# The last four heads' k carried in the padding of the other groups, gathered by GpSimd DMAs, with the loads of w_in on GpSimd and the work in a new order

## The chip, the core and the metric

The kernel runs on one core of one Trainium2 chip. The core has a matrix engine (TensorE, PE in the profile), a vector engine (VectorE, DVE), a scalar engine (ScalarE, ACT), GpSimd (POOL) and SyncE (SP), which here only issues DMAs; 16 DMA engines move the data. The engines run side by side and wait for each other by semaphores. The metric is the device time of one execution in microseconds (us), as the median of several runs.

## What is computed

One token sequence of 2048 tokens with 448 channels (bf16) goes through a block with local attention and then a gated MLP whose gate mixes over the tokens:

```python
qkv = layernorm(x) @ wqkv                    # 448 x 1344; q, k, v of 16 heads, 28 wide
# token s attends to s, s-2, ..., s-14 (8 places, dilation 2)
h = x + softmax(q k^T / sqrt(28)) v @ wo
z = gelu(layernorm(h) @ w_in)                # 448 x 1792
z1, z2 = z[:, :896], layernorm(z[:, 896:])
g = w_sp @ z2 + b_sp                         # w_sp is 2048 x 2048, over the tokens
out = h + (z1 * g) @ w_out                   # 896 x 448
```

## The kernel before

**Stages.** x comes in six loads, is normalised (VectorE: statistics `st`, aggregate `mv`, the product `xn`; GpSimd: the reciprocal root `rs`) and transposed to `xhT`, channels down the partitions: for the first four blocks of 128 tokens on TensorE (`xT0` to `xT3`, copied out of PSUM by `xe`), for the rest by transposing DMAs from SP. From `xhT` TensorE makes q and k (`qk`) and the values (`v`). The attention runs in 18 blocks of some 112 queries: logits (`lg`, two jobs j = 0, 1 of eight heads), exponentials on ScalarE (`ex`), a product with a mask on VectorE (`mk`, line 804), the weighted sum (`o`), its normalisation (`rc`, `om`) and a transposing DMA back (`oT`). Then come the projection (`y`), h, its layer norm, `z2` and `z1`, and from about 121 us on the product with w_sp (`g`, line 950) and the one with w_out (`wo`, line 974).

**q and k.** They are made transposed, in `qkT`: 128 partitions, 8 columns (`gg`) of 2048 tokens. Column 2g holds q and column 2g+1 holds k of the heads 4g to 4g+3; each head has 32 partitions, of which 28 are its channels and 4 are padding. The weights for it, `wqk`, are laid out the same way: copies `wp` (line 514, the helper `move`) put 28 of every 32 columns in place from the raw weights `wraw`, which come in three loads (`wq_0` to `wq_2`), and a GpSimd `memset` (line 678) clears the padding. The tokens are cut in six tiles `QT` of 128, 128, 256, 512, 512 and 512. For each tile and each group g the product `qk{tile}_{g}` makes the two columns 2g and 2g+1 together:

```python
WK = [(0, 1, 2), (0, 3, 2)]
FK = [(0, 2, 3), (0, 1, 3)]
HK = [(1, 0), (2, 64)]
```

The 448 channels are three full chunks of 128 (six matmuls for the two columns, jobs F) and half a chunk of 64 (two matmuls, job H). The two halves use different rows of TensorE and run at the same time. `qe{tile}_{g}` copies the two columns out of PSUM to `qkT`, on ScalarE or VectorE. The logits read them per head:

```python
ins = e.matmul(psum[:, c:c + nq], qkT[p:p + DH, 2 * g + 1, k0:k0 + NK],
               qkT[p:p + DH, 2 * g, t0:t0 + nq], start=True, stop=True,
               tile_position=(p, 0))
```

with p = 32(2j + i), i = 0, 1: job j reads the heads 2j and 2j+1 of every group.

**Order.** Each piece of work is a job with its engine. `ORDER` lists all jobs by number; each engine runs its own jobs in that order, and a wait holds everything behind it on the same engine. `BANK` gives the PSUM bank of each job that needs one, `ON` the engine of each copy. Job 930 (the last number) is a filler: a matmul on constant data (line 989) that keeps TensorE busy while the first data come in. In the order before, SP issues x0, x1, wq_2, wq_0, wq_1, x2, x4, ..., then transposes (about 1.3 us each) with the eight loads of `w_in` between them, then the loads of w_sp. GpSimd runs the setup, the `rs` pairs and small copies `od`.

Of the kernel before, what the change touches and what calls it, by code (L numbers as in the profile page):

```python
# [5 lines left out]
S_TOK = 2048  # L6
D = 448
NHEAD = 16
DH = 28
# [16 lines left out]
ORDER = [1, 114, 23, 28, 5, 930, 930, 29, 4, 930, 930, 24, 930, 2, 930, 930, 3, 37, 25, 930, 39, 930, 6, 930, 930, 40, 930, 9,  # L26
# [65 lines left out]
WLH = [4, 4, 8, 9, 18, 1, 4, 12, 24, 4, 14, 34, 6, 22, 21, 26]  # L92
GRES = 1
WARMT = 9.0
COLD = 6.4
FIRST = [(0, 1), "q", (1, 2), (2, 4), "v", (4, 8), (8, 12), (12, 16), "o"]
LN1G = [(0, 1), (1, 1), (2, 2), (4, 4), (8, 4), (12, 4)]
NF2 = 1
WK = [(0, 1, 2), (0, 3, 2)]
OFF = [0, 128, 192, 320]  # L100
FK = [(0, 2, 3), (0, 1, 3)]
HK = [(1, 0), (2, 64)]
QT = [(0, 128), (128, 256), (256, 512), (512, 1024), (1024, 1536), (1536, 2048)]

# [942 lines left out]
```

## Time and profile before

| | us |
|---|---|
| median of three runs | 242.99 (242.45 to 243.13) |
| the profiled execution | 243.36 |
| its span, first to last instruction | 241.6 |
| TensorE busy | 234.5 |
| VectorE busy | 148.9 |
| ScalarE busy | 92.5 |
| GpSimd busy | 33.3 |

The granted clock of TensorE was full (0.999) over the span. In the page, busy shares over the span come first, then 40 equal slices with one digit per slice (9 is 90% or more), then the DMA queues, then the chain that ended last: from the last instruction back, at each step to what released it. Groups of instructions follow, one line each: engine, operation, output and inputs, shape, count, total busy time, the mean of one in ns, and the idle time before them with what ended it. A row of the timeline has the start, the length, the engine and what ran, and in brackets how long the engine had been idle and what ended that. Rows for DMA issues give the engine that issues, the size and the time from issue to landing. Matmuls are pipelined: the duration of one (379 ns at 512 columns) is longer than the distance to the next.

### The profile page before, as it was taken

To read this page: it belongs to the slowest core of one execution; us is meant where nothing else is said; L and a number is where in the kernel's file an instruction comes from. 1 tells how busy PE (TensorE), PEld (TensorE's weight loads), DVE (VectorE), ACT (ScalarE), POOL (GpSimd) and SP (SyncE) were. 2 spreads that over 40 slices of the span, in tenths; PEclk is the share of its full clock that TensorE was granted. 3 is DMA by queue.
4 is the path that set the end of the run, shared out by engine and by line. 5 is a ranking of instruction groups with operands and counts; after the bars stand their busy time and mean duration, and the time that the engine had idled before them with its cause. 6 is when DMAs were issued, how large, how long until landed. Compare 5 with 4: busy or idle time off the path is not lost.

```text
span 241.6 us, 4270 instructions
## 1 busy us (share of the span) xinstructions
PE 234.5 (97%) x1742; PEld 115.9 (48%) x1759; DVE 148.9 (62%) x321; ACT 92.5 (38%) x116; POOL 33.3 (14%) x76
## 2 busy tenths in 40 slices
PE   7899999999999999999999999999999999999995
PEld 5665454554555554444444444444444444444443
DVE  4899987999886988798793143043109232245264
ACT  4687577884898887859440000000000000000000
POOL 6332202003250210131451000000000000000000
PEclk9999999999999999999999999999999999999999
DMA  6943354536749496889999990000000001100112
GB/s 171 341 120 69 65 109 97 133 87 158 164 87 132 90 136 126 174 137 180 188 199 209 187 171 0 3 0 0 0 3 19 19 1 49 49 0 0 38 60 76
DMA packets 66394, 23.23 MB, mean 96 GB/s; under 512 B 58694, under 2 KB 66246, under 8 KB 66374
## 3 DMA queue, kind: packets, MB, share of 16 engines
q1 hardware_dynamic: 66304, 22.95, 45.8%
q8 instruction: 14, 0.23, 0.4%
q14 instruction: 6, 0.05, 0.1%
q10 hardware_dynamic: 70, 0.00, 0.0%
HBM read 6.84 MB, written 1.84 MB: 36 GB/s over the span
## 4 chain that ended last, share of the span: by engine, by line
PE 92%; DVE 2%; DMA 2%; ACT 1%; SPq 1%; issue 1%; DVEq 0%
PE psum L950 40%; PE psum L498 38%; PE psum L974 9%; PE psum L789 3%; PE psum L813 3%; DMA wraw<-in_A_wqkv_dram 2%; DVE st L616 1%; SPq L529 1%; ACT V L514 0%; ACT E L798 0%; DVE wqk L514 0%; DVE xn L627 0%; DVE mv L618 0%; DVE srg L981 0%; DVE qkT L514 0%
## 5 line engine op out<-in xcount | busy, mean ns | idle before, releaser
L959 DVE TENSOR_TENSOR ub<-psum,bb 128x512 bf16<-128x512 f32 x28 | 19.2, 689 | 56.6 <-PE psum L950 56.1
L950 PE MATMUL psum<-wsp_hi,z2p 128*128 128x512 bf16 x219 | 49.9, 379 | 0.3
L798 ACT ACTIVATE E<-psum 128x896 bf16<-128x896 f32 (+2 forms) x36 | 31.7, 932 | 8.2 <-PE psum L789 8.2
L950 PEld LDWEIGHTS psum<-wsp_hi,z2p 128*128 128x128 bf16 x224 | 21.9, 98 | 26.0
L498 PE MATMUL psum<-xhT,wqk 128*128 128x512 bf16 (+5 forms) x186 | 27.3, 307 | 1.5 <-DVE wqk L514 0.5
L950 PE MATMUL psum<-wsp_lb,z2p 128*128 128x512 bf16 x109 | 25.5, 379 | 0.1
L950 PE MATMUL psum<-wsp_la,z2p 128*128 128x512 bf16 x109 | 25.0, 379 | 0.2
L498 PE MATMUL psum<-w_in,hnT 128*128 128x448 bf16 (+1 forms) x128 | 24.6, 353 | 0.0
L498 PE MATMUL psum<-hnT,w_in 128*128 128x512 bf16 (+1 forms) x112 | 23.8, 380 | 0.0
L974 PE MATMUL psum<-w_out,z1p 128*128 128x448 bf16 (+1 forms) x119 | 22.8, 341 | 0.0
L616 DVE BATCH_NORM_STATS2 st<-x_tm 128x6 f32<-128x448 bf16 x32 | 18.8, 612 | 1.8 <-DMA x_tm<-in_A_x_dram 1.7
L804 DVE TENSOR_TENSOR E<-E,maskb 128x1792 bf16<-128x1792 bf16 (+2 forms) x18 | 19.4, 1092 | 0.7 <-ACT E L798 0.7
L876 DVE BATCH_NORM_STATS2 st<-z2p 128x6 f32<-128x448 bf16 x32 | 18.5, 607 | 1.7 <-ACT z2p L872 1.1
L498 PEld LDWEIGHTS psum<-xhT,wqk 128*128 128x128 bf16 (+1 forms) x192 | 12.7, 97 | 12.9 <-issue 4.1
L981 DVE TENSOR_TENSOR srg<-psum,x_tm 128x448 bf16<-128x448 f32 (+1 forms) x17 | 9.9, 594 | 13.3 <-PE psum L974 7.8
L950 PEld LDWEIGHTS psum<-wsp_la,z2p 128*128 128x128 bf16 x112 | 10.9, 98 | 13.2
L950 PEld LDWEIGHTS psum<-wsp_lb,z2p 128*128 128x128 bf16 x112 | 11.0, 98 | 13.2
L611 POOL TENSOR_TENSOR rs<-rs,negh 128x2 f32<-128x2 f32 (+2 forms) x22 | 16.9, 770 | 1.8
L610 POOL TENSOR_SCALAR rs<-mv 128x2 f32<-128x2 f32 (+2 forms) x22 | 7.7, 352 | 66.3 <-DVE mv L618 47.1
L974 PEld LDWEIGHTS psum<-w_out,z1p 128*128 128x128 bf16 x119 | 11.6, 98 | 10.3
L498 PEld LDWEIGHTS psum<-w_in,hnT 128*128 128x128 bf16 (+1 forms) x128 | 10.4, 97 | 11.8 <-issue 3.0
L917 ACT ACTIVATE z1p<-psum 128x1024 bf16<-128x1024 f32 x14 | 14.1, 1021 | 4.5 <-PE psum L498 4.5
(53 smaller groups left out, 228.6 us busy)
## 6 DMA issues: line engine op xcount, KB each, us to landing
w_in<-in_B_w_in_dram SPq DMA_DIRECT2D x8, 224.0 KB, 3.2
out_dram<-srg SPq DMA_DIRECT2D x16, 112.0 KB, 1.8
x_tm<-in_A_x_dram SPq DMA_DIRECT2D x3, 448.0 KB, 7.1
w_out<-in_B_w_out_dram SPq DMA_DIRECT2D x1, 784.0 KB, 5.6
bb<-in_B_b_sp_dram SPq DMA_DIRECT2D x1, 512.0 KB, 5.2
wraw<-in_A_wqkv_dram SPq DMA_DIRECT2D x2, 224.0 KB, 2.9
wraw<-in_A_wqkv_dram SPq DMA_DIRECT2D x1, 448.0 KB, 5.7
wv<-in_A_wqkv_dram SPq DMA_DIRECT2D x2, 224.0 KB, 6.9
```

Source lines behind the costliest of these rows:

```text
L498: ins = e.matmul(o, w, x, start=g not in seen, stop=left[g] == 0, **kw)
L610: [(lambda e: e.tensor_single_scalar(A, mv[:, m:m + n, 1], EPS, ALU.add), r_mv[k][m:m + n], [rr]), (lambda e: e.tensor_tensor(R, A, negh[: ...
L611: (lambda e: e.tensor_tensor(R, A, negh[:, 0:1].to_broadcast([128, n]), ALU.pow), [rr, r_negh], r_rs[k][m:m + n])],
L616: [(lambda e: e.bn_stats(st[:, m, :], src), [rsrc], [r_st[k][m]])], dve_t(D))
L798: return e.activation(o, i, AF.Exp, scale=SCALE)
L804: return e.tensor_tensor(a, a, maskb[:, 0:1, pad:pad + nq].to_broadcast([NK, NHEAD, nq]), ALU.mult)
L876: [(lambda e, m=m, k=k: e.bn_stats(st3[:, m, k, :], z2p[:, m, D * k:D * (k + 1)]), [r_z2[m]], [r_st[2][m]])], dve_t(D))
L917: return e.activation(o, i, AF.Gelu_apprx_tanh)
L950: ins = e.matmul(psv(tk), z2p[:, s, 128 * fc:128 * fc + 128], w[:, 512 * (tc % 2):512 * (tc % 2) + 512], start=(s == 0), stop=(s == NB - 1))
L959: [(lambda e, tc=tc, s=s, tk=tk: e.tensor_tensor(ub[:, s, :], psv(tk), bb[:, 512 * tc:512 * tc + 512], ALU.add), [r_bb], [r_ub[s]])], dve_ ...
L974: ins = e.matmul(psv(tk, 0, c1 - c0), z1p[:, fc, 128 * m:128 * m + 128], w_out[:, fc, c0:c1], start=(fc == 0), stop=(fc == FC7 - 1))
L981: [(lambda e, m=m, s=s, tk=tk, c0=c0, c1=c1: e.tensor_tensor(srg[:, s, c0:c1], psv(tk, 0, c1 - c0), x_tm[:, m, c0:c1], ALU.add), [r_x[m]], ...
```

## The change

1. The k of the last four heads (group 3, 112 channels) is no longer made in a column of its own. The padding of the other seven columns has 7 x 4 x 4 = 112 places; the weights of those channels are put there by five new copies `wx0` to `wx4` (each for one chunk of input channels), so the products of q and k of the seven columns make them as well. The clearing of the padding on GpSimd goes; a clearing of one half chunk of column 6 on VectorE (`wpad`) comes.
2. Group 3 has then only its q column. Its product `qk{tile}_3F` is four full matmuls, the one over a half chunk having zeros in the other half of its weights; `qe{tile}_3` copies one column.
3. `qkT`'s column 7 is filled by 20 DMAs `kg{i}_{h}`, issued by GpSimd: for each of five groups of tiles `KG` (the first two tiles together) and each of the four rows of heads h, 4 partitions by 7 columns become 28 partitions of column 7. They wait for all copies `qe` of their tiles. Job j of the logits waits for the gathers of h = 2j and 2j+1.
4. The eight loads of `w_in` are issued by GpSimd in place of SP.
5. `ORDER`, `BANK` and `ON` are new throughout. What the texts below use of it: SP starts with x1, x0, x2, wq_2, wq_1, wq_0, x4. TensorE makes all q and k of the tiles 0, 1 and 2 (first `qk0_2`, `qk1_2`, `qk1_0`, `qk0_3`), then `v2` and part of `v0`, and only then the first logits, `lg1_1`; then `lg0_1`, the rest of `v0`, `v4`, `lg1_0`, `lg0_0`, the products of tile 3 with `o1`, and `lg3_0`. VectorE runs, once the weights are there, `wx2`, `wp2_1`, `wp2_0`, the xn of block 2, `wp1_0`, `wp1_1`, `wp0_0`, four statistics and aggregates, two more statistics, and `qe0_0`. ScalarE runs `wx0`, `xe1_0`, `wp0_1`, `xe3_0`, `wp3_0`. GpSimd runs `wx1`, five mask steps, `rs` of the blocks 4 to 7, the gathers 3, 2, 1, 0 of the first group, `rs` of the blocks 8 to 11, and the gathers 1, 3, 2, 0 of the next; the `w_in` loads begin before the gathers of tile 4 and continue among those of tile 5 and the first `rs` of the second layer norm. Several copies `od` go from GpSimd to VectorE.

```diff
-ORDER = [1, 114, 23, 28, 5, 930, 930, 29, 4, 930, 930, 24, 930, 2, 930, 930, 3, 37, 25, 930, 39, 930, 6, 930, 930, 40, 930, 9,
+ORDER = [5, 23, 24, 38, 1, 947, 28, 947, 6, 947, 29, 947, 947, 4, 27, 947, 30, 947, 0, 3, 947, 46, 37, 947, 31, 2, 947, 947,
...
+KG = [[0, 1], [2], [3], [4], [5]]
...
-            [("wv", [128, 4, D], BF16), ("xhT", [128, 4, S_TOK], BF16), ("wqk", [128, 4, 8, 128], BF16)],
+            [("wv", [128, 4, D], BF16), ("xhT", [128, 4, S_TOK], BF16), ("wqk", [128, 4, 7, 128], BF16)],
...
+        r_k3 = [[spot("k3_%d_%d" % (i, h), o_qk, 8 * S_TOK * 2) for h in range(4)] for i in range(len(KG))]
...
-                j_win.append(load("w_in%d_%d" % (c, h), dst, src, [r_wi[-1]], 0.6, (1.4, 1.1), key=1.0 + 0.01 * len(j_win)))
+                j_win.append(load("w_in%d_%d" % (c, h), dst, src, [r_wi[-1]], 1.1, (1.4, 1.1), eng="pool", key=1.0 + 0.01 * len(j_win)))
...
-        pool("wpad", -57.5, [(lambda e: e.memset(wqk[:].rearrange("p c g (h d) -> p (c g h) d", h=4)[:, :, DH:32], 0.0), [], r_pad + r_pad2)], 0.4)
+        pl.job("wpad", "dve", -57.5, [(lambda e: e.memset(wqk[64:128, 3, 6, :], 0.0), [], [r_pad4])], 0.2)
         for g in range(4):
-            for k in range(2):
+            for k in range(2 if g < 3 else 1):
...
+        for c, p0, p1, js in ((0, 0, 128, slice(0, 7)), (1, 0, 128, slice(0, 7)), (2, 0, 128, slice(0, 7)), (3, 0, 64, slice(0, 7)),
+                              (3, 64, 128, slice(1, 7, 2))):
+            i = c + (p0 > 0)
+            move("wx%d" % i, "pool" if p1 - p0 == 128 else "dve", KEY["wp"] + 0.1,
+                 lambda c=c, p0=p0, p1=p1, js=js: wqk[p0:p1, c, :, :].rearrange("p g (h d) -> p g h d", h=4)[:, js, :, DH:32],
+                 lambda c=c, p0=p0, p1=p1, js=js: wraw[p0:p1, c, D + 336:2 * D].rearrange("p (h i g) -> p g h i", h=4, g=7)[:, js],
...
+                    rf = [[r_pad[2 * g]] + r_pad3[0:3] + xr, [r_pad[2 * g + 1], r_pad2[1]] + r_pad3 + xr]
...
+                else:
+                    def fl(e, lo=lo, hi=hi, n=n, tk=tk):
+                        for p, c in ((0, 0), (1, 2), (2, 3), (3, 1)):
+                            ins = e.matmul(psv(tk, 0, n), wap(0, 128, p, 6), xhT[:, c, lo:hi], start=p == 0, stop=p == 3)
+                        return ins
+                    pl.job("qk%d_3F" % t, "pe", key, [(fl, [r_pad[6], r_pad2[0], r_pad4] + r_pad3[0:4] + xr, [])], full_t(n, 4), acq=tk)
...
+        pitch = 8 * S_TOK
+        for ik, tiles in enumerate(KG):
+            lo, hi = QT[tiles[0]][0], QT[tiles[-1]][1]
+            for h in range(4):
+                load("kg%d_%d" % (ik, h),
+                     lambda h=h, lo=lo, hi=hi: bass.AP(qkT[:].tensor, 32 * h * pitch + 7 * S_TOK + lo, [[pitch, DH], [1, hi - lo]]),
+                     lambda h=h, lo=lo, hi=hi: bass.AP(qkT[:].tensor, (32 * h + DH) * pitch + lo, [[pitch, 4], [S_TOK, 7], [1, hi - lo]]),
+                     [r_k3[ik][h]], 1.1, (1.3, 0.15), eng="pool", key=hi / 112.0 + KEY["qe"], reads=[r for t in tiles for r in r_qk[t]])
...
-                lgs[(b, j)] = pl.job("lg%d_%d" % (b, j), "pe", b + KEY["lg"], [(f, rq, [])], 0.2, acq=tk, kind="L", after=[o_jobs.get(b - NE)])
+                lgs[(b, j)] = pl.job("lg%d_%d" % (b, j), "pe", b + KEY["lg"], [(f, rq + rk[2 * j::4] + rk[2 * j + 1::4], [])], 0.2, acq=tk, kind="L", after=[o_jobs.get(b - NE)])
```

More of the change, by code (lines that the diff above doesn't have):

```diff
@@ L674, in wap @@
             return wqk[part0:part0 + np_, c, gg, :]
[L676 to L678 removed]
+        r_pad = [spot("wpad%d" % i, o_wp, 4 * 7 * 256) for i in range(7)]
+        r_pad2 = [spot("wpad2_%d" % i, o_wp, 4 * 7 * 256) for i in range(2)]
+        r_pad3 = [spot("wpad3_%d" % i, o_wp, 4 * 7 * 256) for i in range(5)]
+        r_pad4 = spot("wpad4", o_wp, 4 * 7 * 256)
+        pl.job("wpad", "dve", -57.5, [(lambda e: e.memset(wqk[64:128, 3, 6, :], 0.0), [], [r_pad4])], 0.2)
         for g in range(4):
[L680 removed]
+            for k in range(2 if g < 3 else 1):
                 move("wp%d_%d" % (g, k), "dve", KEY["wp"] + 0.3 * g,
@@ L694, in bass_sequential_preLN__sliding_local_dilated__mixer_gmlp__prompt_kernel @@
                 key = lo / 112.0 + KEY["qk"] + KEY["qkg"] * g
-                tk = Ticket(2)
-                def f(t=t, lo=lo, hi=hi, n=n, g=g, tk=tk):
-                    fs = [[(k, psv(tk, k, n), wap(0, 128, p, 2 * g + k), xhT[:, c, lo:hi], None) for p, c in zip(WK[k], FK[k])]
-                          for k in range(2)]
-                    hs = [(k, psv(tk, k, n), wap(p0, 64, (3, 1)[k], 2 * g + k), xhT[p0:p0 + 64, c, lo:hi], (p0, 0))
-                          for k, (c, p0) in enumerate(HK)]
-                    return fs + [hs] if t < NF2 else [fs[0] + fs[1], hs]
@@ L703, in bass_sequential_preLN__sliding_local_dilated__mixer_gmlp__prompt_kernel @@
-                xr = xh_res(lo, hi)
-                rf = [[r_pad[2 * g]] + xr, [r_pad[2 * g + 1], r_pad2[1]] + xr]
-                product("qk%d_%d" % (t, g), key, f, rf if t < NF2 else rf[0] + rf[1], n, 6, tk, hreads=[r_pad[2 * g + 1], r_pad2[0]] + xr)
-                move("qe%d_%d" % (t, g), "act", lo / 112.0 + KEY["qe"] + KEY["qkg"] * g,
-                     lambda lo=lo, hi=hi, g=g: qkT[:, 2 * g:2 * g + 2, lo:hi],
-                     lambda n=n, tk=tk: psum[:, tk.b * 512:tk.b * 512 + 1024].rearrange("p (k t) -> p k t", k=2)[:, :, 0:n],
-                     [], [r_qk[t][g]], evac_t(2 * n), [tk], tk)
+                nk = 2 if g < 3 else 1
@@ new lines, in bass_sequential_preLN__sliding_local_dilated__mixer_gmlp__prompt_kernel, with f @@
+                tk = Ticket(nk)
+                xr = xh_res(lo, hi)
+                if g < 3:
+                    def f(t=t, lo=lo, hi=hi, n=n, g=g, tk=tk):
+                        fs = [[(k, psv(tk, k, n), wap(0, 128, p, 2 * g + k), xhT[:, c, lo:hi], None) for p, c in zip(WK[k], FK[k])]
+                              for k in range(2)]
+                        hs = [(k, psv(tk, k, n), wap(p0, 64, (3, 1)[k], 2 * g + k), xhT[p0:p0 + 64, c, lo:hi], (p0, 0))
+                              for k, (c, p0) in enumerate(HK)]
+                        return fs + [hs] if t < NF2 else [fs[0] + fs[1], hs]
+                    rf = [[r_pad[2 * g]] + r_pad3[0:3] + xr, [r_pad[2 * g + 1], r_pad2[1]] + r_pad3 + xr]
+                    product("qk%d_%d" % (t, g), key, f, rf if t < NF2 else rf[0] + rf[1], n, 6, tk,
+                            hreads=[r_pad[2 * g + 1], r_pad2[0]] + r_pad3[1:4] + xr)
+                else:
[4 more added lines that the diff above has]
+                    pl.job("qk%d_3F" % t, "pe", key, [(fl, [r_pad[6], r_pad2[0], r_pad4] + r_pad3[0:4] + xr, [])], full_t(n, 4), acq=tk)
@@ new lines, in bass_sequential_preLN__sliding_local_dilated__mixer_gmlp__prompt_kernel @@
+                move("qe%d_%d" % (t, g), "act", lo / 112.0 + KEY["qe"] + KEY["qkg"] * g,
+                     lambda lo=lo, hi=hi, g=g, nk=nk: qkT[:, 2 * g:2 * g + nk, lo:hi],
+                     lambda n=n, nk=nk, tk=tk: psum[:, tk.b * 512:tk.b * 512 + 512 * nk].rearrange("p (k t) -> p k t", k=nk)[:, :, 0:n],
+                     [], [r_qk[t][g]], evac_t(nk * n), [tk], tk)
+        pitch = 8 * S_TOK
[6 more added lines that the diff above has]
+                     [r_k3[ik][h]], 1.1, (1.3, 0.15), eng="pool", key=hi / 112.0 + KEY["qe"], reads=[r for t in tiles for r in r_qk[t]])
@@ L776, in bass_sequential_preLN__sliding_local_dilated__mixer_gmlp__prompt_kernel @@
             slot = b % NE
-            rq = []
+            rq, rk = [], []
             for t, (lo, hi) in enumerate(QT):
@@ L780, in bass_sequential_preLN__sliding_local_dilated__mixer_gmlp__prompt_kernel @@
                     rq += r_qk[t]
+                    for ik, tiles in enumerate(KG):
+                        if t in tiles:
+                            rk += r_k3[ik]
             for j in range(2):
```

27 lines of the change are left out of this document (14 added, 13 removed), and 97 rows, old and new, of tables (BANK, ON, ORDER).

## The prediction

> **What bounds the kernel now.** I read the page first: busy shares, slices, the chain that ended last.
>
> ```profile
> span 241.6 us, 4270 instructions
> PE 234.5 (97%) x1742; PEld 115.9 (48%) x1759; DVE 148.9 (62%) x321; ACT 92.5 (38%) x116; POOL 33.3 (14%) x76
> ...
> PE   7899999999999999999999999999999999999995
> ...
> PE 92%; DVE 2%; DMA 2%; ACT 1%; SPq 1%; issue 1%; DVEq 0%
> ```
>
> TensorE is the bound almost from the first slice to the last; GpSimd has room. A busy TensorE may still run below its peak, so the busy time by stretch comes next, then the order of time on TensorE.
>
> ```profile
> 8.78:22.40 13.62, 13.04 (x201) 8.96 (x202) 13.50 (x37) 11.67 (x22) 3.08 (x7) 1.00 0.60 175
> 22.40:60.00 37.60, 36.77 (x424) 18.39 (x430) 33.64 (x70) 26.39 (x31) 7.22 (x15) 1.00 0.46 101
> 60.00:87.20 27.20, 27.20 (x343) 14.15 (x342) 23.50 (x47) 23.79 (x29) 6.44 (x11) 1.00 0.70 119
> ```
>
> ```profile
> 8.78 0.52 PE L498 MATMUL psum<-xhT,wqk 128*128 128x128 bf16 x6 [0.48 <-DVE wqk L514]
> 9.31 3.39 PE L498 MATMUL psum<-xhT,wqk 128*128 128x128 bf16 x58
> 13.91 1.60 PE L498 MATMUL psum<-wv,xhT 128*128 128x448 bf16 x8 [0.30 <-DVE qkT L514]
> 16.83 2.57 PE L498 MATMUL psum<-xhT,wqk 128*128 128x256 bf16 x22
> 19.23 1.59 PE L498 MATMUL psum<-wv,xhT 128*128 128x448 bf16 x8
> 24.67 2.76 PE L498 MATMUL psum<-xhT,wqk 128*128 128x512 bf16 x12
> 27.27 1.30 PE L498 MATMUL psum<-wv,xhT 128*128 128x448 bf16 x6
> 28.50 0.39 PE L498 MATMUL psum<-xhT,wqk 64*128 64x512 bf16 x2
> ```
>
> The columns after the length of a stretch are TensorE, weight loads, VectorE, ScalarE, GpSimd. TensorE idles 0.6 us in 8.78 to 22.40 and 0.8 us in the next 37.6 us. The other rows give the price of a matmul at full rate: 24.67 to 27.27 is 2.60 us for 12, so 0.217 us at 512 columns. Two 64-row matmuls run side by side and make one "slot". So the 58 from 9.31 (16 of them halves) are 50 slots in 3.39 us, 0.068 each; the 22 from 16.83 to 19.23 (4 halves) are 20 slots in 2.40 us, 0.120 each, changes of mode included. One change: the six 448-wide ones from 27.27 last 6 x 0.189 = 1.13 us by their spacing (1.30 is less a drain), so the halves could start at 28.40 and start at 28.50: 0.10.
>
> **What the change removes.** In each token tile the last product of q and k took 6 full matmuls and a pair of halves, 7 slots; it becomes 4 full ones. Three slots go per tile: two tiles of 128 give 6 x 0.068 = 0.41, one of 256 gives 3 x 0.120 = 0.36, three of 512 give 9 x 0.217 = 1.95; together 2.72 us. The written order has 76 changes of mode where it had 80: 0.40 us. This work lies on the chain, so 3.1 us is the most that TensorE can give. The copies out of PSUM for that group halve; beside copies moved between ScalarE and VectorE that is counted at nothing, as neither ends the chain (2% and 1%). GpSimd's clearing of the padding goes and a small one on VectorE comes, ahead of 8.4 where VectorE waits for the weights: nothing. The order of the later stages is new too, but its matmuls are the same ones, at zero while TensorE stays full there (27.20 of 27.20 above).
>
> **The start.** All products of groups 0 to 2 now also need the carried columns (five copies), and the loads are reordered: a 224 KB load of x goes ahead of the three of q and k weights.
>
> ```profile
> 2.67 5.68 DMA wraw<-in_A_wqkv_dram
> ...
> 8.45 0.80 DVE wqk L514 x4
> ```
>
> ```profile
> 3.15 1.53 SPq L529 DMA_DIRECT2D x_tm<-in_A_x_dram  x3
> ...
> x_tm<-in_A_x_dram SPq DMA_DIRECT2D x1, 224.0 KB, 5.8
> ...
> L616 DVE BATCH_NORM_STATS2 st<-x_tm 128x6 f32<-128x448 bf16 x32 | 18.8, 612 | 1.8 <-DMA x_tm<-in_A_x_dram 1.7
> L627 DVE TENSOR_SCALAR xn<-x_tm,mv,rs 128x512 bf16<-128x512 bf16 x32 | 12.6, 416 | 4.1 <-POOL rs L611 4.1
> L618 DVE BATCH_NORM_AGGREGATE mv<-st 128x2 f32<-128x6 f32 x32 | 4.6, 166 | 0.2
> L514 POOL COPY otm<-otm 112x64 bf16<-112x64 bf16 x6 | 2.5, 424 | 18.8 <-DVE otm L824 18.8
> L514 ACT ACTIVATE wqk<-wraw 128x336 bf16<-128x336 bf16 x4 | 1.7, 473 | 0.6 <-DMA wraw<-in_A_wqkv_dram 0.6
> L514 ACT ACTIVATE xhT<-psum 128x512 bf16<-128x512 f32 x1 | 0.6, 598 | 1.5 <-PE psum L656 1.5
> L514 DVE COPY wqk<-wraw 128x336 bf16<-128x336 bf16 x4 | 0.8, 263 | 1.0 <-DMA wraw<-in_A_wqkv_dram 1.0
> L514 DVE CAST qkT<-psum 128x256 bf16<-128x256 f32 x1 | 0.4, 392 | 0.0
> L611 POOL TENSOR_TENSOR rs<-rs,negh 128x4 f32<-128x4 f32 x3 | 3.1, 1043 | 0.3
> L610 POOL TENSOR_SCALAR rs<-mv 128x4 f32<-128x4 f32 x3 | 0.7, 232 | 13.1 <-DVE mv L618 13.1
> ```
>
> Today the weights are complete at 2.67 + 5.68 = 8.35 and the 224 KB of x behind them land at 3.15 + 5.8 = 8.9. The same bytes stand ahead of the last weights after the change, so I put these at 8.9. Then VectorE copies two pieces (9.4), GpSimd one (its copies take 0.424), ScalarE one: first product at 9.4. Today it starts at 8.78 and has done 6 matmuls (0.41) by 9.31, so the loss is 9.4 - 8.9 = 0.5. On the way the fourth kind of product waits for the seventh VectorE item (six copies of 0.263 and one xn of 0.416 after 8.9: 10.9; TensorE is there after 15 slots, 10.4) and another for the fifth ScalarE item (copies of 0.3 to 0.6; 11.45 against 11.3): 0.65, less the 0.30 wait in the row at 13.91 that goes: net 0.35. With 29 slots more and a transpose (0.23) the first two tiles end at 13.7, the third (25 slots) at 16.7. The v products placed next (8 slots of 0.189, two changes) end at 18.4.
>
> **The gathers, the added wait.** The carried k comes out of PSUM in rows 28 to 31 of each 32; four GpSimd DMAs per tile group bring it to where the logits read it. A logits job waits for two of them, and GpSimd issues them in line. No row shows a DMA issued by GpSimd. The nearest are SP's:
>
> ```profile
> xhT<-xn SPq DMA_TRANSPOSE x12, 2.5
> ...
> L528 SPq DMA_TRANSPOSE xhT<-xn x12: 1189/1264/1297, 15.5 to 41.4; - x12
> ...
> L529 SPq DMA_DIRECT2D w_in<-in_B_w_in_dram x8: 433/578/1449, 33.1 to 58.3; - x8
> L529 SPq DMA_DIRECT2D x_tm<-in_A_x_dram x6: 402/470/897, 0.8 to 7.2; - x6
> ...
> w_in<-in_B_w_in_dram SPq DMA_DIRECT2D x8, 224.0 KB, 3.2
> ```
>
> Bounds: issue 0.40 (fastest load) to 1.45 (slowest), landing after it 1.24 (2.5 - 1.26) to 2.6 (3.2 - 0.58). I take 1.26 and 1.24, the transposes' rows: from SBUF to SBUF like the gathers. VectorE after 10.9: four statistics (0.612) and four aggregates (0.17) to 14.0, two statistics to 15.2, then the cast of a q tile (0.39): 15.6. Only then may the first gather go; GpSimd's own rs work for the next four x tiles (0.23 + 1.04) is done at 15.3. The second gather lands at 15.6 + 2 x 1.26 + 1.24 = 19.4, and the logits could start at 18.4: a stall of 1.0. The cheap bounds give 17.6, no stall.
>
> Later ones are hidden, barely. Third tile: GpSimd ends the first four at 20.6, rs work 21.9, four gathers and a landing: 28.2. TensorE, from 19.4 through logits and two v products (3.5), the 25 slots of the fourth tile (5.4) and outputs and mode changes (0.7), needs it at 29.0. Fourth tile: last copy out of PSUM about 29.7 (0.6 ScalarE), two gathers and landing 33.5, needed at 34.2 (two logits pairs, v, 10 slots of 512, output). Should that cover of 0.7 to 0.8 go, each 0.2 us on a gather counts four times in the third tile. The dear bounds give stalls of 2.8, 0.2 and 1.6 at the three places in place of 1.0: 3.6 us more.
>
> [...]
>
> The eight w_in loads (8 x 0.58 of SP) leave SP, whose transposes otherwise fill it; TensorE's chain names SP for 1%, so nothing is gained. On GpSimd they cost 8 x 1.26 = 10 us, ahead of the fifth tile's gathers and of rs work that has waited for VectorE so far; hidden by GpSimd's 14%, with none of it on the chain.
>
> **Sum.** -2.72 - 0.40 + 0.5 + 0.35 + 1.0 = -1.27 us on the profiled execution of 243.36 us (span 241.6). The median of the runs is 242.99, 0.37 lower; there it gives 241.7.
>
> **Rivals.** *Hidden wholly:* the gathers cost what the cheap bounds say, no stall: 241.7 - 1.0 = 240.7, and 239.9 if the 0.85 of the start goes as well. For: x is ready earlier than before. Against: the queue on VectorE sets 15.6, not the gathers.
>
> *VectorE takes over:* it is busy 13.50 of 13.62 us in the first stretch. If its queue paces the tiles of 512 too, their 1.95 comes back: 243.6, no change. Against: 33.64 of 37.6 later on, and two casts less there.
>
> *VectorE holds GpSimd:*
>
> ```profile
> 34.25 0.24 POOL L514 COPY otm<-otm 112x64 bf16<-112x64 bf16 x1 [4.11 <-DVE otm L824]
> ...
> 40.25 1.35 POOL L514 COPY otm<-otm 112x64 bf16<-112x64 bf16 x1 [5.23 <-DVE otm L824]
> ...
> 40.42 1.08 DVE L804 TENSOR_TENSOR E<-E,maskb 128x1792 bf16<-128x1792 bf16 x1
> ```
>
> The same GpSimd copy takes 0.24 alone and 1.35 where VectorE's mask product runs: it ends when that ends. If a gather's issue is held so, then behind two xn (0.42 each) at 15.6 and a mask product (1.08) in the third tile, whose slack of 0.8 covers most: 0.8 + 0.4 = 1.2 more, 242.9. [...]
>
> *Slower:* issue and landing of GpSimd's DMAs at or beyond the dear bounds. The place is the first logits, then those of tiles three and four. It decides when the pair of gathers takes over 3.76 + 1.27 = 5.0 us from the last copy to landing at the first logits alone, and sooner with the later ones: at 1.45 and 2.6 the time is 241.7 + 3.6 = 245.3; at 2.0 us an issue, with four in line per tile, about 247. For: nothing in the trace shows such an issue cheaper, and 28 of them are added. Against: it needs prices at the far end of the rows.
>
> **Chances.** My forecast 0.38, its own range 240.9 to 242.3 (a stall of 0.2 to 1.6); hidden wholly 0.12; VectorE takes over 0.09; the hold 0.11; slower 0.30. A change under 0.3% (0.73 us) can't be told from none here: faster is the first two, 0.50; same the next two, 0.20; slower 0.30. The range runs from 240.0 (hidden) to 245.5 (the dear bounds), leaving out 0.05 below and 0.13 above.
>
> **What would show it.** Right: 24 full matmuls in place of 36 and 12 halves for the last group; first product near 9.4; a TensorE wait of about 1 us before the first logits, released by a DMA into qkT; issues on GpSimd near 1.3 us. Wrong: a wait on such a DMA again at the third or fourth tile, GpSimd issues far from 1.26, or VectorE as TensorE's releaser through 22 to 60 us.

## The result, and the profile after

The changed kernel takes 244.71 us (median), beside 242.82 for the kernel before in the same runs, 3 us above my forecast of 241.7. The ratio of the means is 1.0094, interval 1.0071 to 1.0118: slower by 0.9%. Of the nine runs eight lie at two levels, 244.2 to 244.7 and 246.2 to 246.4, and one of 248.04 us, at a mean clock of 0.986, is left out of the ratio. What is known of the upper level is told at the end. All comparisons below are such ratios of means to the kernel before in the same batch, with their 95% intervals; one thousandth is 0.24 us. The profiled run is of the lower level (244.37 us, span 242.6).

The page after, as before with TensorE on top:

```profile
span 242.6 us, 4261 instructions
PE 232.1 (96%) x1719; PEld 115.5 (48%) x1735; DVE 149.8 (62%) x326; ACT 92.3 (38%) x119; POOL 49.4 (20%) x100
...
PE 89%; DMA 5%; ACT 2%; DVE 1%; SPq 1%; issue 1%
```

TensorE's busy time fell by 2.4 us (234.5 to 232.1), and the time did not follow: in the chain DMA has 5% where it had 2%. The busy time by stretch (length, TensorE, weight loads, VectorE, ScalarE, GpSimd) says where:

```profile
8.78:22.40 13.62, 11.87 (x142) 7.93 (x144) 12.06 (x36) 8.56 (x18) 9.75 (x18) 1.00 0.65 183
22.40:60.00 37.60, 34.09 (x455) 18.11 (x455) 31.01 (x63) 29.30 (x35) 15.74 (x24) 1.00 0.53 100
60.00:87.20 27.20, 27.02 (x328) 13.96 (x326) 23.44 (x49) 23.43 (x29) 7.95 (x16) 1.00 0.70 116
```

Idle TensorE time is 1.75 us in the first stretch (0.58 before) and 3.5 us in the second (0.83 before). VectorE is not full in either. The last stage, product with w_sp to the end, is the same to a hundredth (117.32 us busy in both, from 122.17 after and 121.20 before), so all of the loss lies ahead of it. TensorE's waits from 8.7 to 70 us, with what the profile names as releaser:

```profile
PE psum L500 <- DMA OT<-otm: 1.6, 1, 1.6
PE psum L820 <- ACT qkT L516: 1.1, 1, 1.1
PE psum L820 <- ACT V L516: 1.0, 1, 1.0
PE psum L500 <- DVE wqk L516: 0.8, 1, 0.8
...
```

From the last row up: the first product (9.45), the first logits that read a gather (18.84), the logits lg5_1 of the fourth tile (35.26, "the fifth logits" below), and an output projection that waits for the transpose oT3 (51.15). The transposes of OT from 40 to 56 us, from issue to landing (shortest, median, longest), first before, then after:

```profile
L528 SPq DMA_TRANSPOSE OT<-otm x5: 1184/1192/1262, 38.8 to 51.3; - x5
...
DMA to landing us min/median/max: 2.4/2.4/4.3
```

```profile
L530 SPq DMA_TRANSPOSE OT<-otm x4: 1187/1462/1857, 43.3 to 55.2; - x4
...
DMA to landing us min/median/max: 3.0/5.8/6.5
```

And the gathers of the fourth token tile, on GpSimd:

```profile
L531 POOL DMA_DIRECT2D qkT<-qkT x4: 587/592/667, 29.7 to 31.6; - x4
...
DMA to landing us min/median/max: 3.2/4.6/4.9
```

An issue costs GpSimd 0.59 us, under half of the 1.26 I took; a landing is 2.6 to 4.3 us behind the issue's end, not 1.24; and transposes that the change does not touch take 5.8 us in place of 2.4. The experiments ask which of this costs what.

### The profile page after: what moved, and what is told of

The parts are those of the page before. It is cut to its first block, busy times and chain, and to the rows that moved or that the text cites. A ratio compares the mean times of both kernels' runs of the same rounds, so it can differ in the third digit from the quotient of the medians.

```text
span 242.6 us, 4261 instructions
## 1 busy us (share of the span) xinstructions
PE 232.1 (96%) x1719; PEld 115.5 (48%) x1735; DVE 149.8 (62%) x326; ACT 92.3 (38%) x119; POOL 49.4 (20%) x100
## 4 chain that ended last, share of the span: by engine, by line
PE 89%; DMA 5%; ACT 2%; DVE 1%; SPq 1%; issue 1%
PE psum L981 40%; PE psum L500 33%; PE psum L1005 9%; PE psum L820 3%; PE psum L844 3%; DMA OT<-otm 3%; DMA wraw<-in_A_wqkv_dram 2%; ACT E L829 1%; PE psum L723 1%; SPq L531 1%; DVE wqk L516 1%; ACT qkT L516 1%; ACT V L516 0%; DVE srg L1012 0%; DVE xn L629 0%
## 5 line engine op out<-in xcount | busy, mean ns | idle before, releaser
L981 PE MATMUL psum<-wsp_hi,z2p 128*128 128x512 bf16 x218 | 49.0, 379 | 0.3
L500 PE MATMUL psum<-xhT,wqk 128*128 128x512 bf16 (+5 forms) x140 | 20.8, 306 | 1.5 <-DVE wqk L516 0.8
L613 POOL TENSOR_TENSOR rs<-rs,negh 128x2 f32<-128x2 f32 (+2 forms) x22 | 19.4, 883 | 1.8
L612 POOL TENSOR_SCALAR rs<-mv 128x2 f32<-128x2 f32 (+2 forms) x22 | 6.7, 304 | 52.8 <-DVE mv L620 34.6
L1005 PEld LDWEIGHTS psum<-w_out,z1p 128*128 128x128 bf16 x119 | 11.6, 98 | 10.3
L500 PE MATMUL psum<-wo,OT 128*128 128x448 bf16 (+1 forms) x64 | 13.1, 353 | 1.6 <-DMA OT<-otm 1.6
```

The source lines that it names most:

```text
L500: ins = e.matmul(o, w, x, start=g not in seen, stop=left[g] == 0, **kw)
L613: (lambda e: e.tensor_tensor(R, A, negh[:, 0:1].to_broadcast([128, n]), ALU.pow), [rr, r_negh], r_rs[k][m:m + n])],
L981: ins = e.matmul(psv(tk), z2p[:, s, 128 * fc:128 * fc + 128], w[:, 512 * (tc % 2):512 * (tc % 2) + 512], start=(s == 0), stop=(s == NB - 1))
L1005: ins = e.matmul(psv(tk, 0, c1 - c0), z1p[:, fc, 128 * m:128 * m + 128], w_out[:, fc, c0:c1], start=(fc == 0), stop=(fc == FC7 - 1))
```

## The experiments

In edits of the written order, job names stand for its numbers: kg*t*_*h* is a gather of tile group *t*, qk, v and lg are the products of q and k, of v, and the logits; xT, oT and hT are SP's transposes.

**w_in back on SP.**

```diff
-j_win.append(load(..., 1.1, (1.4, 1.1), eng="pool", key=...))
+j_win.append(load(..., 1.1, (1.4, 1.1), key=...))
```

> The changed kernel with the eight w_in loads back on SP, at the same places of the order; the gathers stay on GpSimd. Theory one (collision): the burst of w_in loads and gathers that GpSimd issues between 42.7 and 48.0 us is what holds up the transpose oT3 (issued 46.28, landed 51.06) and so TensorE's wait of 1.6 to 1.8 us at 51.2. Without the loads in it the wait goes, and the fourth tile's gathers land within 2 us of their issue: 244.5 - 1.5 = 243.0 us. Theory two (order): the order as rewritten makes the waits, with SP as full as it was; the loads only move back in SP's line, where they cost 8 x 0.58 us beside transposes of 1.26: 244.5 or a little more, 244.3 to 245.5, with a wait for a transpose of OT still near 51 us.

Measured 243.98, ratio 1.0055 (1.0039 to 1.0071), between the two theories: by the ratios 0.95 us of the loss is the w_in loads on GpSimd, with an uncertainty of 0.7. Part of that is the upper level of the changed kernel: its five runs at the lower level have a mean of 244.4, these four 244.0. The wait for oT3 is 0.9 us, not nothing: beside the gathers alone the transposes of OT from 40 to 49 us still take 2.8 to 6.4 us to land. A new wait of 1.2 us stands at 68.03, ahead of the first product with w_in, so the profiled run (244.55) wins nothing.

**No gathers.**

```diff
-qkT[p:p + DH, 2 * g + 1, k0:k0 + NK]
+qkT[p:p + DH, (1, 3, 5, 5)[g], k0:k0 + NK]
...
-[(f, rq + rk[2 * j::4] + rk[2 * j + 1::4], [])]
+[(f, rq, [])]
...
-load("kg%d_%d" % (ik, h), ..., eng="pool", ...)
+pl.job("kg%d_%d" % (ik, h), "pool", 0, [], 0.1)
```

> The changed kernel without its 20 gathers: the last four heads' logits read another k column that is already written (column 5 in place of 7), so their values are left wrong and all other work stays. Theory one (landing): TensorE's waits at 18.84 (1.1 us) and 35.26 (1.25 us) are for the gathers, and some of the wait at 51.15 too: 244.5 - 1.1 - 1.2 = 242.2, down to 241.0 if the transposes near 51 us are on time as well. Theory two (ScalarE): the profile names ScalarE's copies out of PSUM, which end 18.81 and 34.87, as the last releasers; without the gathers these remain and only the 0.3 us between 34.87 and 35.16 is won: 244.2.

Measured 241.82, ratio 0.9954 (0.9934 to 0.9973). The waits at the first and fifth logits are gone, so they were for the gathers, whatever the profile names. Two waits stay: 0.6 us for a transpose of OT, and 1.3 us at 46.08, put down to VectorE. Six w_in loads now go out together at 34.7 to 38.2, and the two xT transposes issued among them take 9.0 and 7.9 us, to 45.7 and 45.9; the product at 46.08 is the first to read them.

**Gathers issued, read by nobody.** The edit of the logits alone, the gathers kept.

> The changed kernel with all its gathers issued, but no logits job reads what they bring (the last four heads read column 5), so their traffic and GpSimd's time stay and only the wait goes. Theory one in its first form (waiting for the landing): the waits at 18.84 and 35.26 go, the one for the transpose at 51.15 stays: 242.2 to 242.8. Theory one in its second form (the transfers hold up other transfers): little goes, 243.8 to 244.5. Theory two (ScalarE): 244.2, like the run without gathers.

Measured 242.65, ratio 1.0009 (0.9985 to 1.0032): the median lies in the range of theory one's first form, but 0.0055 above the run without gathers. The gathers cost while nobody waits for them; the wait for OT is 2.1 us here and 0.6 there.

**The kernel before with w_in on GpSimd.**

```diff
-j_win.append(load(..., 0.6, (1.4, 1.1), key=...))
+j_win.append(load(..., 0.6, (1.4, 1.1), eng="pool", key=...))
```

> The kernel before with nothing changed but the eight w_in loads, which GpSimd issues in place of SP. Theory one: loads from GpSimd land 2.6 to 5.2 us after their issue and hold up the transposes beside them; here they do so without any gather: 0.5 to 1.8 us slower, 243.4 to 244.6. Theory one in the form that the gathers are needed for the collision: 242.8, no change. Rival (SP relief): SP wins 8 x 0.58 = 4.6 us of its line and the transposes go out earlier: 242.3 to 242.8.

Measured 243.79, ratio 1.0034 (1.0012 to 1.0055). No gather is needed for the harm. Its chain around 30 us, in order of time (start, length, what):

```profile
29.98 5.48 DMA OT<-otm
35.46 0.02 issue
35.48 0.64 DVE otm L824
36.12 0.04 issue
36.17 1.04 PE psum L498 x4
```

A transpose of OT, issued 0.2 us behind a w_in load of GpSimd, takes 5.48 us (the same one takes 2.5 in the kernel before); VectorE waits for it to reuse the buffer otm, and TensorE for VectorE to free a PSUM bank.

**Copies and transposes by themselves.** A kernel of six DMAs of a kind per stage; in the stage with both, SP issues six transposes while GpSimd issues six gathers. It was run once.

```diff
+stages = [[("sp", T)], [("pool", G)], [("sp", T), ("pool", G)], [("pool", W)],
+          [("sp", T), ("pool", W)], [("sp", W)], [("sp", "TG")], [("sp", T)]]
```

> A kernel of its own that computes nothing of the reference: it fills buffers, runs eight stages of six DMAs of each named kind, each stage after the one before has landed, and copies the input to the output. Stages: six SP transposes; six GpSimd gathers; both at once; six GpSimd w_in loads; these with six SP transposes; six w_in loads by SP; six transposes and six gathers alternating on SP; six transposes again. Theory one (alternation: a copy and a transpose do not run beside each other, and each change costs): alone, a transpose lands 1.2 us after its issue as in the trace of before and a gather 1.7 to 2.2 us after it; together they take 4 to 6 us, as oT1 and oT3 did in the changed kernel, and the stage with both lasts well over the sum of the two stages alone (over 15 us where each alone is some 6 to 9). Theory two (GpSimd's DMAs are slow to land by themselves): the gathers land 2.6 to 4.6 us after issue in their own stage too, and the transposes beside them keep their 1.2 us.

The transposes alone, beside GpSimd's gathers, beside GpSimd's w_in loads, and alternating with gathers on SP:

```profile
L149 SPq DMA_TRANSPOSE xhT<-xn x6: 1259/1270/1282, 14.6 to 21.2; - x6
...
DMA to landing us min/median/max: 2.5/2.5/2.5
```

```profile
L149 SPq DMA_TRANSPOSE xhT<-xn x6: 1189/1710/2219, 31.0 to 40.2; - x6
...
DMA to landing us min/median/max: 2.5/4.4/7.0
```

```profile
L149 SPq DMA_TRANSPOSE xhT<-xn x6: 1190/1282/3332, 50.7 to 57.7; - x6
...
DMA to landing us min/median/max: 5.1/7.5/9.5
```

```profile
L149 SPq DMA_TRANSPOSE xhT<-xn x6: 1191/1192/1278, 72.6 to 82.6; - x6
...
DMA to landing us min/median/max: 2.5/3.0/3.1
```

The gathers alone, and beside the transposes:

```profile
L154 POOL DMA_DIRECT2D qkT<-qkT x6: 595/595/735, 24.2 to 27.3; - x6
...
DMA to landing us min/median/max: 3.0/3.4/3.4
```

```profile
L154 POOL DMA_DIRECT2D qkT<-qkT x6: 595/595/595, 31.2 to 34.2; - x6
...
DMA to landing us min/median/max: 4.6/5.2/5.7
```

Both theories had a part. A gather takes 3.4 us by itself, some 2.8 of it behind the issue. Beside copies of the other queue a transpose takes 4.4 us (gathers) or 7.5 (w_in loads) in place of 2.5, and the gather 5.2, all medians. The stage with both lasts 12 us against 9 and 7 for the two alone, so as a stream they do not lose: my "well over the sum" was wrong, it is each single transfer that comes late. In one line on SP a transpose takes 3.0. Alone a transpose lands sooner than a gather (2.5 us against 3.4); what makes both late beside another queue no run shows.

**Neither gathers nor w_in on GpSimd.** The edits of the first two runs together.

> The changed kernel without the gathers (the last four heads' logits read column 5 and are left wrong) and with the w_in loads on SP: the shorter products and the new order by themselves. Theory one (alternation): both waits left in the run without gathers (1.5 us at 46.1, 0.75 at 41.0) were made by six w_in loads in a burst that held transposes for 6 to 9 us; they go: 241.8 - 1.8 = 240.0, and no less than 239.6 by the prediction's savings (-2.72 - 0.40 + 0.5 against 242.7 is 240.1). Theory two (the new order is itself at fault): 241.5 to 242.5, with TensorE waits of over 1 us left between 40 and 70 us.

Measured 239.92, ratio 0.9877 (0.9856 to 0.9898), as theory one had it. From 8.5 to 70 us one wait is left:

```profile
PE psum L500 <- DVE wqk L516: 0.4, 1, 0.4
```

The shorter products and the new order by themselves win 3.0 us; all of it, and 2.3 more, is lost to the gathers and to the w_in loads that GpSimd issues.

**w_in early on GpSimd.**

```diff
-kg1_0, ..., w_in1_0, ..., w_in0_1, ..., w_in2_1
+kg1_0, w_in1_0, w_in0_1, w_in1_1, w_in2_0, w_in0_0, w_in3_0, w_in3_1, w_in2_1
```

> The changed kernel with one edit of the order: the eight w_in loads stand on GpSimd right behind the gathers of the third token tile, so that they go out in 22 to 27 us, not in the burst of 43 to 48 us. Theory one (alternation): the stall of 1.8 us at the transpose oT3 shrinks to what the gathers alone make of it (1.07 us in the run with w_in on SP), but the transposes of x that go out at 22 to 28 us now land 4 to 9 us after their issue in place of 1.3 to 3, and the fourth and fifth tile's products wait for them: a new TensorE wait of 1 to 3 us before 36 us, in all 244 to 246. Theory two (only the burst with the gathers hurts): 244.5 - 1.7 = 242.8 and no new wait.

Measured 252.42, ratio 1.0313 (1.0250 to 1.0376). Theory one in kind and too small in size: the xT transposes issued among the loads take 11.6 us (median), and TensorE waits once for 7.6. The granted clock falls in that wait and behind it (0.67 from 30 to 38 us, 0.59 from 38 to 44), which is part of the loss:

```profile
L532 SPq DMA_TRANSPOSE xhT<-xn x4: 1190/1352/2030, 21.6 to 26.2; - x4
...
DMA to landing us min/median/max: 5.3/11.6/12.9
```

**All copies on SP, places unchanged.**

```diff
-(1.3, 0.15), eng="pool", key=hi / 112.0 + KEY["qe"]
+(1.3, 0.15), key=hi / 112.0 + KEY["qe"]
...
-(1.4, 1.1), eng="pool", key=1.0
+(1.4, 1.1), key=1.0
```

> The changed kernel with all gathers and all w_in loads issued by SP in place of GpSimd, at the same places of the order; to be held against the run with the w_in loads on SP (243.98). Theory one (alternation): the same copies change places with the same transposes, so the landings stay at 2 to 5 us; and SP's line now waits for ScalarE's copies of k in front of the transposes behind: 244 to 247. Theory two (GpSimd as the issuer is what is slow): the gathers land as SP's loads do, in 1.2 to 2.6 us, and the stalls of 1.2 us at the first and the fifth logits halve: 242.5 to 243.3.

Measured 249.25, ratio 1.0262 (1.0229 to 1.0294): slower, as theory one said, and above its range. SP's line pays: it stands still for copies of k (3.5 us for ScalarE's, 2.8 for VectorE's), and each gather takes 0.65 us of it, ahead of transposes. TensorE waits 2.0 us for a w_in load, and all four runs have a mean clock of 0.986 or 0.993, so the loss isn't the line alone.

**The v product ahead of the first logits** (w_in on SP).

```diff
-v2H, lg1_1, ve2, lg0_1, v0F
+v2H, v0F, lg1_1, ve2, lg0_1
```

> The run with the w_in loads on SP (243.98) with one edit of the order: the six full matmuls of the first v product (1.13 us) stand ahead of the first logits that read a gather, in place of behind them. The trace names ScalarE's copy of V as what those logits waited for. Theory one (the wait is for the gather, which landed 0.09 us before the logits): the stall of 1.19 us is filled and nothing behind it changes: 242.8 to 243.0. Rival (ScalarE's copy of V is what is waited for, or the gain is given back at the fifth logits): 243.7 to 244.2.

Measured 243.82, ratio 1.0050 (1.0031 to 1.0068): nothing won. Both readings failed. The wait before the logits is filled; but the next product of v now waits 0.6 us at 20.06, just behind the second of two xT transposes, which lands at 19.97, 3.8 us after its issue beside the same gathers (2.5 in the run with neither). That the gather was the releaser, and not ScalarE's copy of V, the run with neither shows: there the same logits start before that copy.

```profile
17.47 0.78 PE L817 MATMUL psum<-qkT 28*128 28x112 bf16 x16
```

```profile
17.58 0.92 ACT L516 ACTIVATE V<-psum 128x896 bf16<-128x896 f32 x1 [1.03 <-PE psum L500]
```

**Gathers of the last three tiles in SP's line** (w_in on SP, v product ahead).

```diff
-(1.3, 0.15), eng="pool", key
+(1.3, 0.15), eng="pool" if ik < 2 else "sp", key
...
-xT12, ..., oT1, kg2_2, ..., kg2_0
+xT12, kg2_3, kg2_2, kg2_1, kg2_0, ..., oT1
...
-kg3_2, ..., oT4, kg3_3, oT3, w_in0_1, ..., kg3_0, ..., kg3_1
+kg3_2, kg3_3, oT4, oT3, kg3_0, kg3_1, w_in0_1
...
-kg4_1, hT2, kg4_0, ..., hT0, w_in2_1, ..., kg4_3, kg4_2
+kg4_1, kg4_0, hT2, ..., hT0, kg4_3, kg4_2, w_in2_1
```

> The changed kernel with the w_in loads on SP, and the gathers of the last three tiles too, each placed in SP's line where their k is ready and where the line has room: four ahead of oT1, two ahead of oT4 and two behind oT3, two ahead of hT2 and two behind hT0; the first two groups of gathers stay on GpSimd. One product of v is done ahead of the first logits that wait for a gather. To be held against the run with the w_in loads on SP (243.98). Theory one, as the run of DMAs alone narrowed it (a transpose is late beside copies of another queue, 3.3 to 8.2 us from the end of its issue to landing, and hardly so when the copies stand in its own line, 1.3 to 2.0): the stalls at the first logits (1.19 us), the fifth logits (1.26), oT3 (1.07) and 68.0 us (1.4) go in most part: 240.2 to 241.5, faster than the kernel before. Rival (SP's line is the bound): the transposes behind the gathers are as late as before, since SP now waits for copies of k and needs 0.65 us for each gather: 243.5 to 246.

**Gathers unread, w_in on SP.** The edits of the first and the third run together.

> The changed kernel with the w_in loads on SP and all gathers issued by GpSimd, but no logits job reads what they bring (the last four heads read column 5 and are left wrong). It stands between the run with gathers waited for (243.98) and the run without them (239.92). Theory one: of the 4.06 us between them the waits for landing at the first and fifth logits are 1.19 + 1.26 = 2.4, and the rest is transposes held up by the gathers' traffic: 241.0 to 241.8, with a TensorE wait for a transpose of OT near 48 us. Rival (the waits for the gathers are all of it): 239.7 to 240.3, no wait for a transpose.

Measured 246.48 (1.0111, 1.0009 to 1.0213) and 247.48 (1.0122, 1.0018 to 1.0226): in both neither theory. The four runs of each spread from 243.6 to 247.6, so the intervals are wide. The waits that I aimed at are gone in the first, or down to 0.7 us and less, and both have a new one of 2.6 to 2.8 us. Here is the chain and the clock of the second:

```profile
61.77 6.05 DMA w_in<-in_B_w_in_dram
67.81 0.45 issue
68.27 0.91 PE psum L500 x2
```

```profile
68.20:71.00 2.80, 2.73 (x16) 1.15 (x18) 0.00 (x0) 0.00 (x0) 0.74 (x2) 0.50 0.49 99
```

The last w_in load stands in SP's line behind two hT transposes, lands at 67.8, and TensorE, now earlier, waits for it. The granted clock is 0.50 in this stretch and 0.61 in the mean of the 4 us behind it. The next runs give that load an earlier place:

```diff
-w_in3_1, ..., hT2, ..., hT0, w_in2_1
+w_in3_1, w_in2_1, ..., hT2, ..., hT0
```

> The run with the gathers of the last three tiles in SP's line (246.48 median, 243.61 in its run at full clock) with one edit: the last w_in load stands right behind the one before it (57.2 us), not behind two hT transposes and four gathers (63.6). Theory one: its landing at 67.15 made the TensorE wait of 2.78 us at 67.7, and the clock fell to 0.65 of full in the 4 us behind that wait; with the load early both go: 243.6 - 2.8 = 240.8, 240.3 to 241.6, faster than the kernel before. Rival (the hT transposes, landed 63.46 and 64.62, or SP's line as a whole are what is late): the wait only changes its releaser, 242.8 to 246.

> The run with the w_in loads on SP and the gathers issued by GpSimd but read by nobody (the last four heads read column 5 and are left wrong), with the last w_in load right behind the one before it. Theory one (the gathers' traffic holds transposes up for about 1 us in all, the rest of the gathers' 4.06 us is waiting): the wait of 2.9 us at 68.3 and the low clock behind it go, the one for a transpose of OT (0.8 to 0.9) stays: 240.5 to 241.2. Rival (traffic is free): 239.6 to 240.2. Rival (traffic holds other transfers up for over 2 us): 242 or more, with a wait near 68 us again.

> All gathers on GpSimd as in the changed kernel, w_in on SP, the v product ahead of the first logits (243.82), and the last w_in load early. It tells how much of the gain of the run with the gathers in SP's line is the load's place alone. Theory one: the wait at 67.6 us (0.65) goes and those at the fifth logits (1.22), at OT (0.55) and at 65.3 (0.81) stay: 242.8 to 243.4. Rival (all that is left is the last load): 241.0 to 242.0.

Gathers in SP's line: 242.66, ratio 1.0000 (0.9987 to 1.0013), 1 to 2 us over theory one, with two waits of 0.5 us left at logits (the first ends 0.14 us after a gather lands, the second is put down to VectorE). Unread: 241.47, ratio 0.9954 (0.9939 to 0.9969), a little over theory one: the gathers without their readers cost 0.0077 over the run with neither, 1.9 us. In the profile two waits are new, 0.4 us at 19.67, behind an xT transpose that lands at 19.58, and this one for OT:

```profile
PE psum L502 <- DMA OT<-otm: 0.8, 1, 0.8
```

They make 1.2 of the 1.3 us between the spans of the two runs (239.6 and 238.3): what the gathers cost here is transposes that come late. All gathers on GpSimd: 244.98, ratio 1.0109 (1.0083 to 1.0135), above both theories and worse than with the load late; the waits at the fifth logits and at 65 us grew. So the load's place alone gains nothing there; where the gathers stand is worth 1.0109 - 1.0000, 2.6 us.

**Both queues at one time, no transpose between.** Of the gathers of each of the last three tiles GpSimd issues two while SP issues two, and SP's transposes come behind.

```diff
-eng="pool" if ik < 2 else "sp"
+eng="pool" if ik < 2 or h in ((0, 1), (0, 1), (2, 3))[ik - 2] else "sp"
...
-kg3_2, kg3_3, oT4, oT3, kg3_0, kg3_1
+kg3_2, kg3_3, kg3_0, kg3_1, oT4, oT3
...
-kg4_1, kg4_0, hT2, ..., hT0, kg4_3, kg4_2
+kg4_1, kg4_0, kg4_3, kg4_2, hT2, ..., hT0
```

> The run with the gathers of the last three tiles in SP's line and the last w_in load early (242.66), with two of each of those four gathers given back to GpSimd, so that SP and GpSimd issue their pairs at the same time and no transpose is issued between them. Theory one (a copy is late where transposes stand among it, whatever engine issues it): the second pairs land 1.3 us or more earlier (they landed 51.27 and 67.24, with waits of 0.69 and 0.67 us for them), the transposes behind start 1.3 us earlier, and both waits go: 241.2 to 241.8. Rival (copies of GpSimd's queue hold up SP's transposes even when they are issued ahead of them): oT3, oT4 and hT land 1 to 2 us later than in that run and make waits of 0.5 us or more each: 242.5 to 244.

Measured 241.51, ratio 0.9950 (0.9935 to 0.9966), theory one by the time, and 0.5% faster than the kernel before: 1.4% faster than the changed kernel, the best version of this study that computes everything. Its mechanism holds in part. The first of the two waits is gone, but TensorE waits 1.0 us at 64.29 for a gather that GpSimd issued at 58.46 and that landed at 64.19 (in the profiled run, the slowest of six). The edit also takes six gathers out of SP's line; what the shorter line gains by itself no run tells. Waits left:

```profile
PE psum L822 <- DMA qkT<-qkT: 1.0, 1, 1.0
PE psum L502 <- issue: 0.7, 1, 0.7
PE psum L502 <- DVE wqk L518: 0.4, 1, 0.4
...
```

The same for the first four gathers, and then also the next four behind xT7 in SP's line:

```diff
-eng="pool" if ik < 2 or h in ((0, 1), (0, 1), (2, 3))[ik - 2] else "sp"
+eng="pool" if ik == 1 or h in (2, 3) and ik in (0, 4) or h in (0, 1) and ik in (2, 3) else "sp"
...
-kg0_3, xT5, ..., kg0_2, xT4, kg0_1, xT6, kg0_0
+kg0_3, kg0_2, kg0_1, kg0_0, xT5, ..., xT4, xT6
```

> The same, with the first four gathers too issued at one time, two by GpSimd and two by SP, ahead of the four xT transposes. Theory one: they land by 17.8 us in place of 18.6 and 19.8, the transposes start 1.2 us later but land 1.3 us after their issue in place of 2.5 to 2.7, and the wait of 0.78 us at 20.3 for them stays or shrinks a little: 0 to 0.4 us below the run before. Rival (the transposes are pushed back by SP's two gathers): the fourth tile's products at 22.6 wait up to 1.2 us more: 0.5 to 1.2 us above the run before.

```diff
-eng="pool" if ik == 1 or h in (2, 3) and ik in (0, 4) or h in (0, 1) and ik in (2, 3) else "sp"
+eng="pool" if h in (2, 3) and ik in (0, 4) or h in (0, 1) and ik in (2, 3) else "sp"
...
-xT7, ..., kg1_1, kg1_3, xT10, kg1_2, xT8, kg1_0
+xT7, kg1_1, kg1_3, kg1_2, kg1_0, ..., xT10, xT8
```

> The run with the first four gathers on both queues at once (244.3 at a clock of 0.992), with the next four in SP's line right behind the transpose xT7, where GpSimd issued them beside it: then xT7 took 2.9 us from the end of its issue to landing (20.40 to 23.30), TensorE waited 2.2 us for it, and the clock fell behind that. Theory one: xT7 lands 1.3 us after its issue, at 21.7; the wait falls to 0.7 us or less, the clock stays full (1.9 us), and the four gathers, needed at 28, have 3 us to spare: 244.3 - 1.6 - 1.9 = 240.8, 240.4 to 241.4. Rival (SP's line): the transposes xT8 to xT11 behind the four gathers, 2.7 us later, make the fifth tile's products wait: 241.8 to 243.5.

244.30, ratio 1.0062 (1.0049 to 1.0075), and 244.13, ratio 1.0045 (1.0026 to 1.0063): both above theory one and above the rival's range. In the first, where it goes the rival's way, GpSimd's two gathers land by 17.1 and the first three transposes take 2.5 us again, but xT7, the last transpose that the fourth tile needs, is issued behind two gathers of SP and then beside the next ones of GpSimd (start, length, what):

```profile
19.13 4.17 DMA xhT<-xn
...
23.43 0.59 PE psum L502
```

In the second TensorE still waits 1.5 us for xT7, which takes 3.4 us and not 2.5, and 1.2 us at 36.39 for gathers of the fourth tile; the fifth tile's products, which the rival named, do not wait. None of the three places tried for the first eight gathers was free of a wait.

## Why the prediction was wrong

The forecast was -1.27 us and the ratio gives +2.28. By the ratios, each times 242.8: the products and the order -2.99 us (run with neither), the gathers unread +1.87, waiting for the gathers at most +2.45 (1.0055 - 0.9954), w_in on GpSimd +0.95. These are steps from run to run, so they add up by construction; each is uncertain by 0.5 to 0.7. The 2.45 holds more than waiting, since its two runs differ also in the last load's place: the run with gathers read has 2.1 us of waits at the first and the fifth logits, and the 1.2 us at 68.03, put down to ScalarE's copy of V, with the last w_in load landed at 67.6. With that load late in both, the unread run (1.0122, wide interval) is not faster than the read one at all. Against the sum, 1.87 and 0.95 are terms that stood at nothing, waiting is up to 1.45 over its 1.0, and the rest is 0.72 better; that makes the 3.55 us between forecast and measurement. The prediction's terms stand against these.

- **What the change removes** (-2.72 - 0.40): right in kind, and not measured by itself. With the start and the new copies (+0.5 + 0.35) the sum was -2.27; measured -2.99. The first product starts at 9.45 (forecast 9.4), but the 0.35 us of waiting for copies is not there: the third tile ends at 16.1 against my 16.7.
- **The first logits** (+1.0): right in size by luck, a wait of 1.0 us at 18.84: two errors cancel. Two issues and a landing are 4.0 us (14.73 to 18.75), I had 3.76; but the issues are 0.6 to 0.8 us, not 1.26, and the landing 2.4, not 1.24. In the kernel of DMAs alone a gather takes 3.0 to 3.4 us with nothing beside it.
- **"Later ones are hidden, barely"**: the step that failed first. The third tile is hidden (landed 23.9, needed at 28.7). The fourth is not: the pair that the fifth logits need lands at 35.16, I had 33.5, against a need at 34.2, as forecast: a wait of 1.1 us in place of a cover of 0.7. I gave all gathers the landing of a transpose that runs alone. These wait among xT and oT transposes and take up to 4.9 us from issue.
- **What lies beside the gathers**: missing from the sum. I asked what waits for a gather and not which other transfers it delays. oT3's wait of 1.6 us is the largest of all, and the unread gathers cost 1.9 us with no one waiting for them, and in the profile 1.2 of 1.3 us of that are waits for transposes.
- **"w_in on GpSimd: hidden by GpSimd's 14%"**: wrong, some 0.95 us here (by ratios whose difference is uncertain by 0.7) and 0.8 us alone in the kernel before (0.3 to 1.3). The idle share of the issuing engine was the wrong cover. On SP each load stands between transposes; on GpSimd five go out within 4.2 us here and six within 3.5 without the gathers, and SP's transposes are among them. Their own landing went from 3.2 (median) to 5.3 us.
- **The rivals**: "slower" was the side that came, and named tile four, but not at its prices: issues were cheap (0.59 to 0.81 us; no gather of the changed kernel took the 1.45 or 2.0 that it priced), and it had nothing on held transposes. VectorE did not take over (31.0 of 37.6 us). The hold did not come as priced: the first gathers' issues took up to 0.81 us against 0.59 in the later ones, 0.2 us and not a whole instruction of VectorE's.

Still open: why one burst makes transposes take 7 us and another 12, and how the 2.45 us divide between landing, the last load's place and the clock.

## What to carry to other kernels

Moving a DMA to an idle engine's queue moves it in time as well: ask which transfers of the other queue it will stand among, and price those at their late landing (here 4 to 12 us for a transpose of 2.5), not the issue alone. An unread version (transfer kept, waiting cut) beside a version without it tells traffic from waiting in two runs, if no new wait comes in: here one of the three unread runs met one of 2.8 us, at a load that now came too late. Where a wait's named releaser ended in the same tenth of a microsecond as a DMA landed, take the DMA away before believing the name.

## What the runs showed of the hardware

In these runs a TensorE wait of 2.0 us or more came with a lower granted clock, and so cost more than itself. In the profiled runs whose longest TensorE wait from 8.5 to 80 us is 1.6 us or less, the mean granted clock is full (0.999 or 1.000). In the six with a longer one it is not: 0.993 with 2.0 us (all copies on SP), 0.993 with 2.1 (gathers unread), 0.992 with 2.2 (first gathers on both queues), 0.993 with 2.6 (gathers in SP's line), 0.986 with 2.8 (unread, w_in on SP) and 0.980 with 7.6 (w_in early). In the 3.8 us behind the 2.1 us wait the mean is 0.57 of full clock, from 68 to 72 us behind the one of 2.6 it is 0.65. Behind the 2.2 us wait:

```profile
23.40:26.50 3.10, 3.06 (x8) 1.17 (x9) 1.23 (x1) 0.27 (x1) 0.98 (x1) 0.50 0.43 86
```

The clock is 0.50 of full for 3.1 us, and all five of its runs have a mean clock of 0.992 or 0.993, which over 242 us is 1.8 us. Behind the changed kernel's wait of 1.6 us the profile shows full clock; two of its three runs at 246 us have 0.992 or 0.993, the third a full mean clock, so for that one the level stays unexplained.
